# Score matmuls of batches 1 to 3 with a head's q and k on all 128 partitions

## The chip, the cores and the metric

One core of a Trainium2 chip runs one launch. The metric is the device time of the launch in microseconds. Engines are named as the profile names them: PE (matmuls) with PEld (its weight loads), DVE, ACT, POOL, and SP, which only issues DMAs.

## What is computed

Causal attention over 4 batches, 8 heads, 576 tokens, head size 64, all in fp32, with a bias made of running sums, and after it two feed-forward stages over all 2304 tokens:

```python
scores = 0.125 * q @ k.T
cum = np.cumsum(np.maximum(s, 0), axis=-1)
scores = where(causal, -1e9, scores + np.minimum(cum[..., None, :] - cum[..., :, None], 0))
x = softmax(scores) @ v            # heads side by side: 2304 x 512
h = x @ w_in;  x = (h - tanh(h)) @ w_out                 # 512 -> 2048 -> 512
x = ((x @ w1) * (x @ w2)) @ w3 @ w_o2                    # 512 -> 1024 -> 1024 -> 512
```

An fp32 product is made of fp32r matmuls: each operand is cut into a high part (fp32r) and a low part (what is left), and high x high, high x low and low x high are added up in PSUM. In batch 0 the scores are plain fp32 matmuls instead.

## The kernel before

Attention goes by pairs of heads. The two heads of a pair lie on partitions 0 to 63 and 64 to 127, so that one tile `qk` (128 x 2 x 576: q, then k) holds a pair. In batches 1 to 3 each pair of heads is worked off as an early pair (kind A, the first 256 queries, one unit) and a late pair (kind B, the other 320 queries, three units B1, B2, B3); both share one load of q and k. Twelve such couples follow each other. The table `UNITS` (L135) lists what a unit multiplies: A has 128 queries by 128 keys and 128 by 256; B1 and B2 each 96 queries by 512 keys; B3 128 by 384 and 96 by 64.

The order of PE's instructions is written out by hand. `at(step, order, fn)` puts a piece of work into a step, and within a step the pieces come by their order number. A unit's scores have order 4 (L512), its row minimum on DVE order 1 and its exponentials on ACT order 2.5 of the next step; transposes, copies out of PSUM and the products with v follow 7 to 9 steps later. A couple takes 8 steps; its A unit is at step k0, B1 at k0+2, B2 at k0+4, B3 at k0+6. After the attention work of a step come pieces of the first feed-forward stage (`ffn`, its `h` at L452 and `y` at L431), paced so that they fill PE until the next tokens are there. DVE and ACT run in an order that a scheduler chooses, in which `in_turn` keeps some pieces behind others.

For a couple in batches 1 to 3:
- `load` (L170) brings q and k with one DMA of 576 KB on SP's queue, at step k0-6 (L532), held back by `paced` (L148) until the last score matmul before it has ended. It goes into one of five buffers with the tag "raw", taken in turn.
- `cut` (L175) makes the high part on ACT (L178) and the low part on DVE (L179), each with one instruction over 2 x 576 columns, at step k0-3 with order 5.7 (L536). They take two more of the five buffers.
- `scores` (L221) goes for each rectangle of the unit over three passes (high x high, high x low, low x high) and in each over the two heads (L229). Each matmul has 64 rows: head 0 on partitions 0 to 63, head 1 on 64 to 127, into two PSUM banks.

The rings of PSUM banks (`ps_a`, five banks), the biases (`bias`, L192; loaded by `load_cum`, L187, at step k0-5) and everything after the scores stay as they are. Work that the scores share DVE and ACT with: the row minimum (L268), the exponentials (L290), the conversions of weights (`plain`, L84; `park`, L103) and the cutting of the feed-forward input (`cut_x`, L407).

Of the kernel before, what the change touches and what calls it, by code (L numbers as in the profile page):

```python
# [8 lines left out]
F32 = mybir.dt.float32  # L9
F32R = mybir.dt.float32r  # L10
# [5 lines left out]
P = 128  # L16
B, H, S, D = 4, 8, 576, 64
# [7 lines left out]
BLK = 256  # L25
NB = NT // BLK
NSLOT = 16
NP = NH // 2
TAIL = S - BLK

CH0 = [0, 128, 256, 384, 480]
PW = [128, 128, 128, 96, 96]
# [2 lines left out]


@with_exitstack
def tile_kernel(ctx: ExitStack, tc: tile.TileContext, qk, v, s, w_in, w_out, w1, w2, w3t, w_o2, outT):
    nc = tc.nc
    PSUM = bass.MemoryType.PSUM  # L40

# [38 lines left out]
    def in_turn(i, behind):  # L80
        if behind is not None:
            tc.add_manual_dep(i.ins, behind.ins.name, mybir.DependencyInfo(mybir.DependencyClass.NoSync, mybir.DependencyReason.SCHED_ONLY))
# [40 lines left out]
    with ExitStack() as actx:  # L123
        def pool(name, bufs, **kw):
            return actx.enter_context(tc.tile_pool(name=name, bufs=bufs, **kw))

        f2 = pool("f2", 2, reuse_waits="tile")
        a2 = pool("a2", 2, reuse_waits="tile")
# [6 lines left out]
        UNITS = {"A": ((0, 0, P, 0), (1, 0, BLK, P)), "B1": ((3, 0, 512, 0),), "B2": ((4, 0, 512, 0),),  # L135
                 "B3": ((2, 0, 384, 0), (4, 512, S, 384))}
# [8 lines left out]
        latest, least, last_exp, paces = [None], [None], [None], []  # L145
        PACED = 70

        def paced(i):  # L148

            if latest[0] is not None and len(paces) < PACED:  # L150
                paces.append(i)
                tc.add_manual_dep(i.ins, latest[0].ins.name, mybir.DependencyInfo(mybir.DependencyClass.Sync, mybir.DependencyReason.DATA))
            return i

        class Pair:


# [10 lines left out]
                self.nm = self.sums = None  # L168

            def load(self):  # L170
                self.raw = a2.tile([P, 2, S], F32, tag="raw", name=f"qk{self.n}", bufs=5)
                w = BLK if self.first and self.early else S
                return paced(nc.sync.dma_start(self.raw[:, :, :w], qk[self.id, :, :, :w]))

            def cut(self, other):  # L175

                hi, lo = (a2.tile([P, 2, S], F32R, tag="raw", name=f"qk{z}{self.n}", bufs=5) for z in "hl")
                in_turn(nc.scalar.copy(hi, self.raw), last_exp[0])  # L178
                in_turn(nc.vector.tensor_sub(lo, self.raw, hi.bitcast(F32)), least[0])  # L179
                self.hl = other.hl = hi, lo  # L180

            def load_v(self):
                self.vs = a2.tile([P, 2, 5, D], F32, tag="vs", name=f"vs{self.n}", bufs=3)
# [37 lines left out]
        def scores(p, j):  # L221
            ps = [ps_a.tile([P, 512], F32, tag="s", name=f"s{p.n}_{j}_{e}") for e in range(2)]
            p.banks[j] = ps
            for i, k0, k1, o in UNITS[j]:
                passes = ((p.raw, p.raw),) if p.first else ((p.hl[0], p.hl[0]), (p.hl[0], p.hl[1]), (p.hl[1], p.hl[0]))
                for z, (w, x) in enumerate(passes):
                    for e in range(2):
                        r = slice(D * e, D * e + D)
                        latest[0] = nc.tensor.matmul(ps[e][:PW[i], o:o + k1 - k0], w[r, 0, CH0[i]:CH0[i] + PW[i]], x[r, 1, k0:k1],  # L229
                                                     start=z == 0 and (not p.first or (i, k0, k1, o) == UNITS[j][0]),  # L230
                                                     stop=not p.first and z == 2, skip_group_check=True)
            if p.first:


                for e in range(2):
                    g = p.g[e]
                    todo = []
                    for i, k0, k1, o in UNITS[j]:
                        z, r = REL[i]
                        pw, d = PW[i], max(k0, CH0[i])  # L240
                        todo.append((ps[e][:pw, o:o + k1 - k0], pick[:, g:g + 1].broadcast_to([P, pw]), rel2[z][:, r + k0:r + k1]))
                        if d < k1:
                            todo.append((ps[e][:pw, o + d - k0:o + k1 - k0], identb[:, :pw], maskb[:, d - CH0[i]:k1 - CH0[i]]))
                    for z, (o, w, x) in enumerate(todo):
                        nc.tensor.matmul(o, w, x, start=False, stop=z == len(todo) - 1, skip_group_check=True)
# [242 lines left out]
        pairs = [Pair(n, *x) for n, x in enumerate(order)]  # L488
        when = {}

        def at(step, order, fn, *args):
            when.setdefault(step, []).append((order, len(when.get(step, ())), fn, args))
# [8 lines left out]
        start = -2  # L501
        k, avail = 0, []
        for p in pairs:
            n, k0 = p.n, k
            lag = 5 if p.first and p.early else 7
            for m, j in enumerate(p.units):
                k = k0 + 2 * m
                for i in NEED[j]:
                    at(max(k - 2, start), 5, bias, p, i)
                    if not p.first:  # L510
                        at(max(k - 1, start + 1), 0.2, causal, p, i)
                at(k, 4, scores, p, j)  # L512
                at(k + 1, 1, minimum, p, j)
                at(k + 1, 2.5, exps, p, j)
                for e in range(2):
                    at(k + e + lag, 2, transposes, p, j, e)
                    at(k + e + lag + 1, 1.5, evacuate, p, j, e)
                at(k + lag + 2, 8, products, p, j)
            ke = k0 + 2 * len(p.units) - 2
            k = ke + 2  # L520
            at(ke + 2, 5.5, invert, p)
            at(ke + 5, 2.4, turn, p)
            at(ke + 6, 1.2, store, p)
            at(ke + 6, 3.9, spread, p)
            fin = ke + lag + (5 if p.first and p.early else 3)
            at(fin, 2.6, finish, p)
            if p.hp == H // 2 - 1:
                avail.append((S * p.b + (BLK if p.early else S), fin))

            if n > 1 and (p.early or p.first):  # L530
                q = p if p.first else pairs[n + 1]
                at(max(k0 - 6, start + 1), 4.2, load, p, q, "load")  # L532
                at(max(k0 - 2, start + 1), 4.3, load, p, q, "load_v")
                if not p.first:
                    at(k0 - 5, 4.4, load, p, pairs[n + 1], "load_cum")
                    at(k0 - 3, 5.7, p.cut, pairs[n + 1])  # L536


        begin = [next(a for q, a in avail if q >= BLK * (k + 1)) for k in range(NB)]
        step_of, t = [], 0  # L540
        for k in range(NB):
            for i in range(4 * F1):
                t = max(t, begin[k])
# [66 lines left out]
        k = start  # L610
# [227 lines left out]
    for n, f in enumerate(W3ORDER):  # L838
# [3 lines left out]
        ps = ps3.tile([P, 512], F32, tag=f"o{n % 2}", name=f"w3o{f}")  # L842
# [25 lines left out]
    def bank(tag, name, bufs=1):  # L868
        return ps3.tile([P, 512], F32, tag=tag, name=name, bufs=bufs)
# [78 lines left out]
    for u, (sb, f) in enumerate(units):  # L948
# [4 lines left out]
        wu, b = wts.pop(u), bs[sb]  # L953
        nxt = u + 1 < len(units)
        w = bank("W", f"W_{u}", 2)
# [103 lines left out]
```

## Time and profile before

| | |
|---|---|
| time, median of 3 runs | 928.15 us (927.96 to 929.91) |
| the profiled execution | 930.37 us, of which the span of its instructions is 928.6 us |
| PE busy in the span | 913.7 us (98%) |
| PEld, DVE, ACT, POOL | 799.8, 654.3, 447.8, 166.0 us |
| score matmuls of batches 1 to 3 | 87.2 to 334 us of the span |
| granted TensorE clock, mean | 0.998 |

A row of the timeline has the start in us from the start of the span, the time of the group in us, engine, line, operation, tiles, shape and count. The profile draws a matmul from its issue to its modelled end, so that matmuls overlap on PE; what a stream of them takes is read from start to start.

### The profile page before, as it was taken

What the parts mean: (1) busy time and instruction counts of PE and PEld (TensorE: products, weight loads), DVE (VectorE), ACT (ScalarE), POOL (GpSimd) and SP (SyncE); (2) the same over time, 40 slices, a digit from 0 to 9 for tenths busy, and PEclk for the clock granted to TensorE, in tenths of its full rate; (3) what the DMA queues carried; (4) which work ended last, traced back from release to release, by engine and by line L of the source; (5) the groups of instructions that cost most, each with busy time, mean ns of one, the idle gap of its engine ahead of it and who ended that gap; (6) DMA issues with size and microseconds to landing.
All of it is one profiled execution on the core that took longest, in us unless ns stands there. A gap on an engine that the chain in (4) does not pass through costs nothing.

```text
span 928.6 us, 16365 instructions
## 1 busy us (share of the span) xinstructions
PE 913.7 (98%) x6031; PEld 799.8 (86%) x6034; DVE 654.3 (70%) x1445; ACT 447.8 (48%) x1047; POOL 166.0 (18%) x170
## 2 busy tenths in 40 slices
PE   8999999999999999999999999999999999999998
PEld 5567887888888889998888888898999999999998
DVE  8888797877878766867897885767245647564555
ACT  4558888767776743324532342335224333433133
POOL 2015646545344300000000000000011111111100
PEclk9999999999999999999999999999999999999999
DMA  5655365445443523499786635346399777777874
GB/s 162 199 184 167 125 232 189 151 155 163 150 171 126 193 84 100 148 353 378 274 288 228 213 110 164 121 173 223 109 320 316 306 253 284 273 267 257 279 271 151
DMA packets 59936, 192.92 MB, mean 208 GB/s; under 512 B 6640, under 2 KB 21136, under 8 KB 55760
## 3 DMA queue, kind: packets, MB, share of 16 engines
q1 hardware_dynamic: 59856, 191.88, 59.9%
q8 instruction: 47, 0.77, 0.3%
q14 instruction: 33, 0.27, 0.1%
HBM read 148.71 MB, written 43.15 MB: 207 GB/s over the span
## 4 chain that ended last, share of the span: by engine, by line
PE 76%; DMA 4%; DVE 4%; ACT 1%; issue 1%; SPq 0%; DVEq 0%; ACTq 0%
PE W L864 10%; PE y L431 9%; PE h L117 9%; PE yb L117 9%; PE hb L117 8%; PE oW L927 5%; PE Y L864 5%; PE w3o L117 5%; PE oY L927 4%; PE pv L327 3%; PE pt_B L301 2%; PE s_B L229 2%; PE V L864 2%; DMA raw_w<-in_w3t 2%; PE s_A L229 1%
## 5 line engine op out<-in xcount | busy, mean ns | idle before, releaser
L117 PE MATMUL h<-xhl,win 128*128 128x256 f32 x864 | 120.7, 286 | 4.0 <-DVE xhl L65 2.9
L117 PEld LDWEIGHTS h<-xhl,win 128*128 128x128 f32 x864 | 105.9, 188 | 14.5 <-DVE xhl L65 3.6
L117 PE MATMUL hb<-x,win 128*128 128x512 f32 (+1 forms) x480 | 104.6, 367 | 0.0
L117 PEld LDWEIGHTS hb<-x,win 128*128 128x128 f32 x480 | 83.9, 188 | 14.9
L117 PE MATMUL yb<-ghb,wout 128*128 128x512 f32 (+1 forms) x320 | 96.1, 368 | 0.7 <-ACT ghb L64 0.5
L997 POOL TENSOR_TENSOR xy<-c,c 128x384 f32<-128x384 f32 x12 | 15.4, 1279 | 445.1 <-DVE c L986 445.1
L206 POOL TENSOR_SCALAR pr<-cb,cq 128x384 f32<-128x384 f32 (+1 forms) x48 | 91.2, 1912 | 13.4 <-PE s_B L229 7.6
L431 PE MATMUL y<-gh,wout 128*128 128x256 f32 x576 | 86.1, 290 | 0.4 <-DVE gh L64 0.4
L290 ACT ACTIVATE pr<-pr,nm 128x128 f32<-128x128 f32 (+2 forms) x120 | 71.4, 597 | 20.8 <-DVE nm L268 20.7
L431 PEld LDWEIGHTS y<-gh,wout 128*128 128x128 f32 x576 | 73.3, 191 | 3.6 <-issue 2.0
L117 PEld LDWEIGHTS yb<-ghb,wout 128*128 128x128 f32 x320 | 58.2, 188 | 11.2 <-ACT ghb L64 1.3
L117 PE MATMUL yb<-glb,wout 128*128 128x512 f32 (+1 forms) x160 | 58.6, 368 | 0.2 <-DVE glb L65 0.2
L301 PE MATMUL pt_B<-ident,pr 96*128 96x96 f32 (+1 forms) x384 | 51.6, 257 | 0.1
L268 DVE CUSTOM_DVE_ANT_0 pr<-s_B,pr 96x512 f32<-96x512 f32 (+1 forms) x72 | 44.4, 637 | 9.3 <-PE s_B L229 8.3
L218 POOL TENSOR_SCALAR_AFFINE_SELECT pr<-pr 128x256 f32<-128x256 f32 (+2 forms) x60 | 30.0, 520 | 98.3 <-issue 97.8
L64 ACT CAST ghb<-thb 128x512 fp32r<-128x512 f32 (+1 forms) x40 | 23.1, 579 | 50.3 <-DVE thb L726 50.3
L310 ACT COPY pf_B<-pt_B 128x512 f32<-128x512 f32 (+2 forms) x72 | 35.8, 499 | 20.9 <-PE pt_B L301 20.6
L460 ACT ACTIVATE th<-h 128x256 f32<-128x256 f32 x72 | 26.9, 374 | 38.7 <-PE h L117 37.6
L431 PE MATMUL y<-gl,wout 128*128 128x256 f32 x288 | 45.2, 280 | 0.0
L301 PEld LDWEIGHTS pt_B<-ident,pr 96*128 96x128 f32 (+1 forms) x384 | 41.1, 142 | 4.4 <-issue 3.0
L875 ACT COPY s<-Y 128x384 f32<-128x384 f32 x24 | 11.6, 482 | 63.6 <-PE Y L864 61.1
L463 DVE TENSOR_TENSOR th<-h,th 128x256 f32<-128x256 f32 x72 | 30.0, 416 | 15.0 <-ACT th L460 14.3
(217 smaller groups left out, 2045.1 us busy)
## 6 DMA issues: line engine op xcount, KB each, us to landing
S<-wg_d SPq DMA_DIRECT2D x24, 1024.0 KB
wo<-wo_d SPq DMA_DIRECT2D x42, 512.0 KB
A<-wg_d SPq DMA_DIRECT2D x24, 768.0 KB
qk<-in_qk SPq DMA_DIRECT2D x16, 576.0 KB
raw_win<-in_w_in SPq DMA_DIRECT2D x16, 512.0 KB
raw_wout<-in_w_out SPq DMA_DIRECT2D x16, 512.0 KB
raw_w<-in_w SPq DMA_DIRECT2D x16, 512.0 KB
wg_d<-pks SPq DMA_DIRECT2D x8, 1024.0 KB
```

The costliest lines, as they stand in the source:

```text
L117: i = nc.tensor.matmul(ps, a, b, start=first and n == 0, stop=last and n == 2, skip_group_check=skip)
L206: nc.gpsimd.tensor_scalar(out=t[:pw, e, :w], in0=p.cb[:pw, e, :w], scalar1=c, scalar2=0.0, op0=ALU.add, op1=ALU.min)
L218: nc.gpsimd.affine_select(out=dg, in_=dg, pattern=[[0, 2], [-1, w - c]], compare_op=ALU.is_ge, fill=-8e9, base=0, channel_multiplier=1)
L268: least[0] = nc.vector.tensor_tensor_reduce(out=t[:pw, k0:k1], in0=ps[:pw, o:o + k1 - k0], in1=t[:pw, k0:k1], scale=-0.125, scalar=nm[:pw, ...
L290: last_exp[0] = nc.scalar.activation(t[:pw, :], t[:pw, :], AF.Exp, bias=m, scale=-1.0, accum_out=p.sums[:pw, e, c:c + 1])
L301: nc.tensor.transpose(pt[:, at:at + pw], p.pr[i][:pw, e, KC0[kj]:KC0[kj] + P], ident[:pw, :pw])
L310: (nc.vector.tensor_copy if j == "B2" and not p.first else nc.scalar.copy)(pf[:, :at], pt[:, :at])
L327: nc.tensor.matmul(p.pv[D * e:D * e + D, c:p.nq], p.vs[:, e, kj], pf[:, beg:end], start=z == 0, stop=z == len(todo) - 1, skip_group_check= ...
L431: nc.tensor.matmul(o, wout[f][:, z, P * c:P * c + P], x, start=f == 0 and n == 0 and c % 2 == 0, stop=f == F1 - 1 and n == 2, skip_group_c ...
L463: nc.vector.tensor_sub(t, hh, t)
L864: i = nc.tensor.matmul(ps[:, :T], w[:, x, P * j:P * j + P], b[:, y, j], start=first and j == n == 0, stop=stop and j == 1 and n == 2, skip ...
L927: nc.tensor.matmul(ps[:, :T], w[:, a, q % 2, P * j:P * j + P], x[:, b, q], start=o in ("B11", "B21", "T1") and q == z == 0, stop=o in ("T4 ...
```

## The change

The host lays out a second input `qd` for batches 1 to 3: for each pair of heads and for q and k one array of 128 x 2 x 576, in which head e stands in [:, e, :], its 64 rows twice, on partitions 0 to 63 and again on 64 to 127. `load` brings q and k in two DMAs of 576 KB into the tiles `qr` and `kr`. `cut` makes three tiles: `qh` (high part of q, on both halves), `ql` (low part of q, on both halves) and `ks` (high part of k on partitions 0 to 63, low part on 64 to 127; ACT writes the high part on all partitions, then DVE puts the low part over the upper half). A matmul of all 128 rows of `qh` with `ks` gives high x high plus high x low; one of `ql` with `ks` gives low x high plus low x low. Each head and rectangle has these two matmuls. The five tiles have one buffer each. The cut goes in two parts: columns 0 to 255 at step k0-2, and columns 256 to 575 at step k0, both with order 5.7.

```diff
-                self.raw = a2.tile([P, 2, S], F32, tag="raw", name=f"qk{self.n}", bufs=5)
-                w = BLK if self.first and self.early else S
+                if not self.first:
+                    self.raw = [place(t, f"{t}{self.n}") for t in ("qr", "kr")]
+                    for z, t in enumerate(self.raw):
+                        i = paced(nc.sync.dma_start(t, qd[self.id - H // 2, z]))
+                    return i
+                self.raw = place(("qr", "kr", "qh", "ks", "ql")[self.n % 5], f"qk{self.n}")
+                w = BLK if self.early else S
...
-            def cut(self, other):
-                hi, lo = (a2.tile([P, 2, S], F32R, tag="raw", name=f"qk{z}{self.n}", bufs=5) for z in "hl")
-                in_turn(nc.scalar.copy(hi, self.raw), last_exp[0])
-                in_turn(nc.vector.tensor_sub(lo, self.raw, hi.bitcast(F32)), least[0])
-                self.hl = other.hl = hi, lo
+            def cut(self, other, a, b):
+                (qr, kr), c = self.raw, slice(a, b)
+                if not a:
+                    self.hl = other.hl = [place(t, f"{t}{self.n}", F32R) for t in ("qh", "ks", "ql")]
+                qh, ks, ql = self.hl
+                in_turn(nc.scalar.copy(qh[:, :, c], qr[:, :, c]), last_exp[0])
+                in_turn(nc.vector.tensor_sub(ql[:, :, c], qr[:, :, c], qh[:, :, c].bitcast(F32)), least[0])
+                in_turn(nc.scalar.copy(ks[:, :, c], kr[:, :, c]), last_exp[0])
+                in_turn(nc.vector.tensor_sub(ks[D:, :, c], kr[D:, :, c], ks[D:, :, c].bitcast(F32)), least[0])
...
+                    for z in (0, 2):
+                        latest[0] = nc.tensor.matmul(ps[e][:PW[i], o:o + k1 - k0], p.hl[z][:, e, CH0[i]:CH0[i] + PW[i]], p.hl[1][:, e, k0:k1],
+                                                     start=z == 0, stop=z == 2, skip_group_check=True)
...
-                    at(k0 - 3, 5.7, p.cut, pairs[n + 1])
+                    at(k0 - 2, 5.7, p.cut, pairs[n + 1], 0, BLK)
+                    at(k0, 5.7, p.cut, pairs[n + 1], BLK, S)
```

`place` takes a tile of 128 x 2 x 576 with one buffer under the given tag. Batch 0 keeps its scores; its pairs take the same five places in turn.

## Rows read from the trace of the kernel before

**Rows 1.** Page, part 1: busy time, share of the span, instructions.
```profile
PE 913.7 (98%) x6031; PEld 799.8 (86%) x6034; DVE 654.3 (70%) x1445; ACT 447.8 (48%) x1047; POOL 166.0 (18%) x170
```
**Rows 2.** Windows of one couple: length, busy PE PEld DVE ACT POOL, clock, DMA; sum.
```profile
162.40:186.40 24.00, 22.54 (x182) 19.03 (x180) 20.08 (x60) 17.72 (x49) 12.73 (x12) 0.93 0.44 146
...
sum 252.80, PE 249.71 PEld 209.46 DVE 200.47 ACT 188.81 POOL 120.03; mean PE 20.81 PEld 17.45 DVE 16.71 ACT 15.73 POOL 10.00
```
**Rows 3.** Waits of PE, 20 to 345 us: total us, times, longest.
```profile
PE h L117 <- DVE xhl L65: 2.9, 2, 1.5
```
**Rows 4.** Timeline of PE around a unit B2 and a unit B3.
```profile
97.44 0.52 PE L301 MATMUL pt_B<-ident,pr 128*128 128x128 f32 x4
97.90 0.48 PE L229 MATMUL s_B<-qkh 64*96 64x512 f32 x2
98.21 0.40 PE L229 MATMUL s_B<-qkl,qkh 64*96 64x512 f32 x2
98.45 0.40 PE L229 MATMUL s_B<-qkh,qkl 64*96 64x512 f32 x2
98.78 0.97 PE L431 MATMUL y<-gh,wout 128*128 128x256 f32 x6
...
101.05 0.44 PE L229 MATMUL s_B<-qkh 64*128 64x384 f32 x2
...
101.70 0.25 PE L229 MATMUL s_B<-qkl,qkh 64*96 64x64 f32 x2
101.78 0.25 PE L229 MATMUL s_B<-qkh,qkl 64*96 64x64 f32 x2
101.97 1.69 PE L117 MATMUL h<-xhl,win 128*128 128x256 f32 x12
```
**Rows 5.** Timeline of PE around a unit A, in two windows.
```profile
208.25 0.33 PE L229 MATMUL s_A<-qkh 64*128 64x128 f32 x2
...
208.53 0.27 PE L229 MATMUL s_A<-qkh,qkl 64*128 64x128 f32 x2
...
209.13 0.38 PE L117 MATMUL h<-xhl,win 128*128 128x256 f32 x1
...
209.35 1.46 PE L117 MATMUL h<-xhl,win 128*128 128x256 f32 x11
210.65 0.60 PE L301 MATMUL pt_B<-ident,pr 128*128 128x128 f32 x5
211.04 1.17 PE L431 MATMUL y<-gh,wout 128*128 128x256 f32 x8
```
**Rows 6.** Timeline of PE: streams of 128-row matmuls in later stages.
```profile
449.98 2.88 PE L117 MATMUL hb<-x,win 128*128 128x512 f32 x12
452.70 0.39 PE L117 MATMUL yb<-ghb,wout 128*128 128x512 f32 x1
...
700.43 1.20 PE L864 MATMUL Y<-B22hl,S 128*128 128x384 f32 x6
701.47 0.85 PE L864 MATMUL W<-T3hl,S 128*128 128x384 f32 x4
```
**Rows 7.** Groups: busy us, mean ns of one, idle before, its releaser.
```profile
L178 ACT CAST qkh<-qk 128x1152 fp32r<-128x1152 f32 x12 | 13.8, 1154 | 7.6 <-DMA qk<-in_qk 7.6
L179 DVE TENSOR_TENSOR qkl<-qk,qkh 128x1152 fp32r<-128x1152 f32 x12 | 16.2, 1350 | 0.0
...
L64 ACT CAST ghb<-thb 128x512 fp32r<-128x512 f32 x32 | 19.9, 622 | 45.0 <-DVE thb L726 45.0
...
L65 DVE TENSOR_TENSOR glb<-thb,ghb 128x512 fp32r<-128x512 f32 x32 | 22.0, 688 | 6.5 <-ACT ghb L64 6.2
```
**Rows 8.** Windows between units: A to B1 (first, last), B3 to A (middle).
```profile
163.30:166.80 3.50, 3.50 (x34) 2.92 (x32) 3.43 (x16) 1.93 (x8) 2.66 (x5) 1.00 0.02 5
290.35:296.37 6.02, 6.02 (x53) 4.70 (x51) 4.43 (x16) 4.43 (x12) 6.02 (x4) 1.00 0.68 235
297.25:302.10 4.85, 4.85 (x44) 4.29 (x42) 4.62 (x19) 3.74 (x13) 1.15 (x5) 1.00 0.01 3
```

More of the change, by code (lines that the diff above doesn't have):

```diff
@@ L37, in tile_kernel @@
 @with_exitstack
-def tile_kernel(ctx: ExitStack, tc: tile.TileContext, qk, v, s, w_in, w_out, w1, w2, w3t, w_o2, outT):
+def tile_kernel(ctx: ExitStack, tc: tile.TileContext, qk, qd, v, s, w_in, w_out, w1, w2, w3t, w_o2, outT):
     nc = tc.nc
@@ L153, in paced, with place @@
             return i
+        def place(tag, name, dt=F32):
+            return a2.tile([P, 2, S], dt, tag=tag, name=name, bufs=1)
         class Pair:
@@ L224, in scores @@
             for i, k0, k1, o in UNITS[j]:
-                passes = ((p.raw, p.raw),) if p.first else ((p.hl[0], p.hl[0]), (p.hl[0], p.hl[1]), (p.hl[1], p.hl[0]))
-                for z, (w, x) in enumerate(passes):
-                    for e in range(2):
+                for e in range(2):
+                    if p.first:
                         r = slice(D * e, D * e + D)
-                        latest[0] = nc.tensor.matmul(ps[e][:PW[i], o:o + k1 - k0], w[r, 0, CH0[i]:CH0[i] + PW[i]], x[r, 1, k0:k1],
-                                                     start=z == 0 and (not p.first or (i, k0, k1, o) == UNITS[j][0]),
-                                                     stop=not p.first and z == 2, skip_group_check=True)
+                        latest[0] = nc.tensor.matmul(ps[e][:PW[i], o:o + k1 - k0], p.raw[r, 0, CH0[i]:CH0[i] + PW[i]], p.raw[r, 1, k0:k1],
+                                                     start=(i, k0, k1, o) == UNITS[j][0], stop=False, skip_group_check=True)
+                        continue
+                    for z in (0, 2):
+                        latest[0] = nc.tensor.matmul(ps[e][:PW[i], o:o + k1 - k0], p.hl[z][:, e, CH0[i]:CH0[i] + PW[i]], p.hl[1][:, e, k0:k1],
+                                                     start=z == 0, stop=z == 2, skip_group_check=True)
             if p.first:
@@ L1039 @@
     qk = np.stack([q, k], axis=2).reshape(NP, 2, 2, S, D).transpose(0, 1, 4, 2, 3)
+    qd = np.stack([q, k], axis=1).reshape(B, 2, H // 2, 2, S, D)[1:].transpose(0, 2, 1, 5, 3, 4).reshape(NP - H // 2, 2, D, 2, S)
     arrays = {
         "qk": np.ascontiguousarray(qk).reshape(NP, P, 2, S),
+        "qd": np.ascontiguousarray(np.stack([qd, qd], axis=2)).reshape(NP - H // 2, 2, P, 2, S),
         "v": vp,
```

## Prediction

> **What bounds the kernel now.** I read the page first: PE is busy 913.7 of 928.6 us, no other engine above 71% beside its own weight loads [rows 1]. Then the windows by couple, over the stretch that the change touches: in 252.8 us PE is busy 249.7, DVE 200.5, ACT 188.8 [rows 2]. PE is the bound here, its order is written by hand, and a microsecond of PE time saved is a microsecond of the span so long as the others keep up. DVE keeps 52 us free there, ACT 64. PE's few waits show what happens where they don't: the longest (1.5 us, for DVE's cut of the feed-forward input) [rows 3] lies in the couple in which PE is busy 22.54 of 24.00 us and the mean granted clock is 0.93 [rows 2]. A stretch there ran at the lower level, 1.2 instead of 2.4 GHz, after PE had stood idle. Seven per cent of 24 us is 1.7 us lost beside the wait. Last the timeline of PE: what a unit's scores really take.
>
> **How the scores run now.** In B2 the three passes start at 97.90, 98.21 and 98.45 us, two matmuls in each [rows 4]. So a pass of both heads takes 0.24 us, and one matmul of 512 columns over all 128 rows takes 2.72/12 = 0.227 us [rows 6]. The two heads, on different halves of the array, run side by side: a pass of two costs what one full matmul costs.
>
> The Trainium skill, TensorEngine Tiling (Array Packing), section Performance Considerations, advises just this for a contraction of 64 rows or less: tile the rows, two matmuls at once. The trace agrees inside the unit. By that rule alone the change is a loss: four matmuls one after the other where there were three passes. Its time is worked out as a rival below.
>
> But the halves have an edge. Four transposes ahead of B2 take 97.44 to 97.90, 0.46 us [rows 4]; five ahead of full matmuls take 210.65 to 211.04, 0.39 [rows 5]. One transpose is some 0.08 (0.39/5), so going to half-array matmuls costs 0.46 - 4 x 0.08 - the same 0.03 or so, thus **0.15 us**, taken low 0.12. At the other end the last pass of B2 takes 98.45 to 98.78, 0.33 instead of 0.24 (in the block below), and the first full matmul after a unit 209.13 to 209.35, 0.22, where the next eleven take 1.30/11 = 0.118 [rows 5]: **0.10 us** more. The same page (section Key Properties) says that a change of tiling mode drains the engine. These rows fit that, though they show the time and not its cause.
>
> **PE, step by step.** Before, a unit costs 0.15 (entry) + its block from its first score to the next work + 0.10 (exit). Blocks: B1 and B2 0.88, B3 0.92 (101.05 to 101.97) [rows 4], A 0.88 (208.25 to 209.13) [rows 5]. That makes 1.13, 1.13, 1.17 and 1.13 us.
> After, all matmuls around are full ones and entry and exit fall away. What stays is the longer first interval after transposes, 0.07 (0.31 against 0.24 in B2 [rows 4]). Prices from start to start: 512 columns 0.227, 384 columns 1.04/6 = 0.173 [rows 6], 256 columns 0.118 [rows 5]. Two operations have no full-array row. For 128 columns the three passes of A go from 208.25 to 208.53, 0.28; less 0.07, that is 0.105 each [rows 5]. For 64 columns the pass from 101.70 to 101.78 gives 0.08 [rows 4]. I take both; they could be as low as 0.06 and 0.04 if the columns alone counted (by the 0.118 of 256), and as high as 0.118 each.
> - B1, B2: 4 x 0.227 + 0.07 = 0.98, saves 0.15 each.
> - B3: 4 x 0.173 + 4 x 0.08 + 0.07 = 1.08, saves 0.09.
> - A: 4 x 0.118 + 4 x 0.105 + 0.07 = 0.96, saves 0.17.
>
> Together 0.56 a couple, twelve couples: **-6.7 us**. Rounding of starts to 0.01 us, and the low entry of 0.12, put it between -5.3 and -7; with the first interval's 0.07 gone too (48 x 0.07 = 3.4) and the small matmuls at their lowest (12 x 4 x 0.085 = 4.1) the far end is -14, with them at their highest (12 x 4 x 0.05 = 2.4) the near end is -2.9. I take -6.5.
>
> **ACT and DVE.** The cut now goes over q and k twice. ACT: 512 columns 0.622 us, 1152 columns 1.154 [rows 7], so 0.83 ns a column and 0.73 us for 640. Two of each are 2.70 instead of 1.15: +1.55 x 12 = **+18.6 us on ACT**. DVE: 0.688 and 1.350 [rows 7], 0.82 for 640, 3.02 instead of 1.35: **+20 us on DVE** (half of its instructions go over 64 partitions, which I count as no cheaper). Both fit into the 64 and 52 us that are free, so the sum puts them at nothing; the cover is that slack, and in places it is thin.
>
> **Waits that the change adds.** With one buffer, part 1 of the cut (256 columns of each head) cannot start before B3 of the couple before has left the three tiles, and A waits for it. The chain is ACT 0.62, ACT 0.62, DVE 0.69 = 1.93 us, in a stretch of 6.02 in which ACT and DVE each have 1.59 free [rows 8]: the added 1.24 and 1.38 fit. Part 2 (320 columns) comes after A and B1 waits for it: 0.73 + 0.73 + 0.82 = 2.28 us, in 4.85 with DVE 4.62 busy, and at the tightest 3.50 with DVE 3.43 [rows 8]. Here 1.64 us of DVE work finds 0.23 or 0.07 free. Behind the waiting instructions on DVE stand A's row minimum, which frees PSUM banks, and the conversions, which can wait. Since the cut is issued ahead of the conversions of its step, I expect it to push those back and PE to be held seldom. If nothing gave way, B1 would be late by 1.64 - 0.23 = 1.4 us, twelve times: 17 us. If everything did, nothing. I take **+2 us**, near the lower end since the chain of 2.28 fits twice into 4.85; that is one late B1 in nine, or one of 1.5 us with the clock's 1.7 on top.
>
> **DMA and SP.** Twelve more DMAs of 576 KB: at 146 GB/s for a share of 0.44 [rows 2] the full rate is some 330 GB/s, so 1.7 us each. The load still goes at k0-6, the first part needs it at k0-2 instead of k0-3; a step is about 2.6 us (252.8/96 [rows 2]), so the later step pays for it. ACT waited 7.6 us in all for these loads [rows 7], and that wait goes. Late next is the bias of the couple, queued behind: 1.7 us later, ACT waits there. Counted at nothing on PE for the same slack, at most part of the 17 us above.
>
> **Sum.** -6.5 + 2 = -4.5 us. The profiled execution took 930.37 us, 0.24% over the median of 928.15; the saving carries over, so about 925.9 there and **923.7 us** as the median.
>
> **Rivals.**
> 1. *The cut becomes the wait* (slower). Place: B1, behind part 2 of the cut on DVE, in the stretch from A. For it: DVE is 95% busy there [rows 8]. Against: conversions can be pushed back, and DVE is only 79% busy over all. Price: up to 17 us, so 928.15 - 6.5 + 17 = 939. It decides from 6.5/12 = 0.54 us a couple on. Chance 0.14.
> 2. *Side by side is worth more than the edges cost* (slower). If what entry and exit cost belongs to the scores and not to the halves, 0.25 stays in each unit, and a fourth matmul comes on top: B1, B2 +0.23 each, B3 +0.25, A +0.22, together 0.93 x 12 = 11 us: 939. This is what the skill's advice gives. Against: the exit of full matmuls to full matmuls costs nothing extra in the streams [rows 6]. Chance 0.05.
> 3. *The gain is taken back* by small waits of PE on DVE, ACT or PSUM banks: 6.5 us lost over 24 parts of a cut, 0.27 each: 926.3 to 930, no change. Chance 0.19.
> 4. *It doesn't do what it says* (the cut parts queue so that both A and B1 see the old rhythm, PE idles at unchanged step times): the same time as 3, counted there.
>
> **Numbers.** My forecast, faster by over 0.2% (1.9 us, about what a measurement of this kernel can tell from no change), has 0.62, from 918 to 926 by itself. No change 0.19, slower 0.19 (rivals 1 and 2). To leave out no more than 2 in 10, the range goes from 919 to 932: below lie the lowest prices of the small matmuls, above the harder half of rivals 1 and 2.
>
> **What the profile would show.** Right: score matmuls 128 rows high, starting one by one; B1's block near 0.98 us; the first matmul after a unit as quick as the second; PE's windows over the twelve couples shorter by 5 to 7 us; DVE busy near 220 us there, ACT near 207. Wrong: PE waiting at s_B or s_A for DVE's `ks` or `ql`, at transposes for a copy that ACT made late, a second stretch at the lower clock, or full-array scores that keep an entry of 0.15 us.

## The result, and the profile after

The changed kernel takes **938.84 us** (median of 6 runs, 934.76 to 942.48); the kernel before took 927.54 beside it (6 runs, 925.57 to 929.91). The ratio is 1.0115, 95% interval 1.0096 to 1.0133: **slower by 10.7 us**, where 4.5 us faster was forecast. The profiled execution has a span of 937.9 us against 928.6.

The page's first part, of the changed kernel: PE is busy as long as before [rows 1], DVE 20 us and ACT 15 us longer.

```profile
PE 913.0 (97%) x5890; PEld 810.8 (86%) x5890; DVE 674.0 (72%) x1481; ACT 463.1 (49%) x1083; POOL 172.1 (18%) x170
```

The stretch from the first to the last score matmul of batches 1 to 3, as windows (length, busy PE PEld DVE ACT POOL, granted clock, DMA share, GB/s). First the kernel before:

```profile
87.20:333.90 246.70, 243.60 (x2115) 204.63 (x2116) 198.72 (x604) 185.72 (x510) 120.03 (x120) 0.99 0.47 159
```

And the changed kernel; the last two are two short windows in its third couple:

```profile
86.50:344.20 257.70, 244.63 (x1971) 215.39 (x1971) 218.87 (x639) 200.19 (x545) 127.65 (x121) 0.98 0.52 177
129.00:132.00 3.00, 0.06 (x1) 0.09 (x2) 1.43 (x4) 3.00 (x9) 3.00 (x2) 0.94 0.51 135
131.60:135.10 3.50, 3.16 (x16) 3.19 (x17) 3.37 (x8) 2.13 (x6) 3.50 (x3) 0.51 0.44 157
```

The stretch is 11.0 us longer, more than the whole loss of the profiled execution. PE stands idle 13.1 us in it (257.70 - 244.63) instead of 3.1. And the clock costs more: after the idle of 3 us at 129 the next 3.5 us ran at 0.51, the level of 1.2 GHz. Two more stretches of the changed kernel ran at that level, each after PE had stood idle in places; the kernel before had one. First the one of before, then the two:

```profile
171.00:174.40 3.40, 3.40 (x19) 3.40 (x18) 1.64 (x4) 1.89 (x6) 0.00 (x0) 0.50 0.94 330
```
```profile
179.40:182.80 3.40, 3.40 (x20) 3.40 (x19) 1.74 (x5) 1.76 (x5) 0.00 (x0) 0.51 1.03 411
...
261.40:264.80 3.40, 3.23 (x15) 3.24 (x16) 3.30 (x6) 2.67 (x7) 3.40 (x6) 0.50 0.54 161
```

At half the full clock, 3.4 us cost 1.7 us of work: 1.7 us lost before, 5.1 after.

Now the score matmuls themselves, in the timeline of PE (two windows of the changed kernel), to be held against [rows 4] and [rows 5]:

```profile
96.54 0.53 PE L315 MATMUL pt_B<-ident,pr 128*128 128x128 f32 x4
96.85 0.45 PE L244 MATMUL s_B<-ks,qh 128*96 128x512 f32 x1
97.14 0.39 PE L244 MATMUL s_B<-ks,ql 128*96 128x512 f32 x1
97.36 0.39 PE L244 MATMUL s_B<-ks,qh 128*96 128x512 f32 x1
97.59 0.40 PE L244 MATMUL s_B<-ks,ql 128*96 128x512 f32 x1
97.82 0.85 PE L445 MATMUL y<-gh,wout 128*128 128x256 f32 x6
...
99.83 0.42 PE L244 MATMUL s_B<-ks,qh 128*128 128x384 f32 x1
...
100.90 1.66 PE L117 MATMUL h<-xhl,win 128*128 128x256 f32 x12
102.40 0.49 PE L315 MATMUL pt_A<-ident,pr 128*128 128x128 f32 x3
...
107.24 0.33 PE L244 MATMUL s_A<-ks,qh 128*128 128x128 f32 x1 [0.92 <-DVE ks L192]
107.40 0.28 PE L244 MATMUL s_A<-ks,ql 128*128 128x128 f32 x1
107.52 0.28 PE L244 MATMUL s_A<-ks,qh 128*128 128x128 f32 x1
...
108.27 0.39 PE L445 MATMUL y<-gh,wout 128*128 128x256 f32 x2
```

The entry is gone: four transposes ahead of B2 take 0.31 us (96.54 to 96.85) instead of 0.46. B2's block is 0.97 (0.98 forecast), B3's 1.07 (1.08), A's 1.03 (0.96). Only after B3 a little of the exit stays: twelve `h` take 1.50 us from 100.90 to 102.40, 0.08 more than twelve at 0.118. So a couple saves 0.16 in B1 and in B2, 0.02 in B3 and 0.10 in A, some **5 us** for twelve. PE got what it was to get. The waits and the clock took it, and twice as much again.

What PE waited for, from the first score to the last (total us, times, longest):

```profile
PE pt_B L315 <- DVE xy L378: 3.0, 1, 3.0
PE h L117 <- DVE xhl L65: 2.8, 3, 1.1
PE s_A L244 <- DVE ks L192: 2.7, 3, 0.9
PE h L117 <- DVE th L477: 2.0, 3, 0.9
```

One wait of 3.0 us, the others at most 1.1, and only 2.7 us of them for the cut itself. The wait of 0.92 us at 107.24 (second couple) comes behind a slow instruction on DVE, whose `ql` of 512 columns took 1.25 us there and 0.68 to 0.69 elsewhere at its fastest:

```profile
105.22 1.25 DVE L190 TENSOR_TENSOR ql<-qr,qh 128x512 fp32r<-128x512 f32 x1
106.50 0.69 DVE L192 TENSOR_TENSOR ks<-kr,ks 64x512 fp32r<-64x512 f32 x1
```

What the others waited for, in the same stretch:

```profile
POOL pr L218 <- DMA cb<-cum_d: 49.0, 5, 14.6
...
ACT pr L220 <- DMA cb<-cum_d: 11.0, 8, 3.3
...
SPq L177 <- PE s_B L244: 35.0, 10, 4.8
SPq L177 <- DVE ql L190: 30.6, 7, 6.1
```

Before, ACT waited 3.0 us for the couple's bias `cb`, and POOL did not wait for it. The 49 us are not new idle time, though: all of POOL's waits together are 119.5 us now and 112.8 before, then put down to other releasers. The same holds for SP's queue, which stands at the load of q and k (L177) for 65.6 us, 30.6 of them put down to DVE's reading of the old tiles. Before, it stood at that load nearly as long, for PE alone:

```profile
SPq L173 <- PE s_B L229: 59.6, 10, 9.6
```

`paced` holds the load until the last score matmul of B1 anyway, and DVE had read the old tiles by then. One couple, from that matmul to the first reading of the bias, before and after:

```profile
131.08 0.40 PE L229 MATMUL s_B<-qkh,qkl 64*96 64x512 f32 x2
131.55 0.33 SPq L173 DMA_DIRECT2D qk<-in_qk  x1
131.97 0.38 SPq L190 DMA_DIRECT2D cb<-cum_d  x1
136.73 1.50 ACT L208 ACTIVATE pr<-cb,cq 128x256 f32<-128x256 f32 x4 [0.25 <-DMA cb<-cum_d]
```
```profile
137.84 0.39 PE L244 MATMUL s_B<-ks,ql 128*96 128x512 f32 x1
138.25 0.33 SPq L177 DMA_DIRECT2D qr<-in_qd  x1
138.63 0.42 SPq L177 DMA_DIRECT2D kr<-in_qd  x1
139.16 0.38 SPq L202 DMA_DIRECT2D cb<-cum_d  x1
144.89 1.50 ACT L220 ACTIVATE pr<-cb,cq 128x256 f32<-128x256 f32 x4 [1.19 <-DMA cb<-cum_d]
```

The load goes out within 0.1 us of the matmul's end in all of eleven couples before and in ten of eleven after; in the eleventh it is 1.45 us late, and the queue had stood at a store of converted weights (L106) just ahead of it. So the single buffers hold the queue in none. The bias lands late all the same, since one more load is issued and moved ahead of it: 8.4 us after that matmul instead of 6.6, as means over the eleven couples.

DVE's and ACT's cut, by shape (line, operation, count, busy, mean ns, idle before), against [rows 7]:

```profile
L190 DVE TENSOR_TENSOR ql<-qr,qh 128x640 fp32r<-128x640 f32 x12 | 11.6, 966 | 0.1
L192 DVE TENSOR_TENSOR ks<-kr,ks 64x512 fp32r<-64x512 f32 x12 | 10.8, 902 | 0.4
L192 DVE TENSOR_TENSOR ks<-kr,ks 64x640 fp32r<-64x640 f32 x12 | 10.8, 897 | 0.4
L190 DVE TENSOR_TENSOR ql<-qr,qh 128x512 fp32r<-128x512 f32 x12 | 10.1, 844 | 4.7 <-ACT qh L189 4.7
```

DVE spends 43.3 us on it instead of 16.2: +27, where +20 was reckoned. ACT spends 32.0 us on its 48 instructions instead of 13.8: +18.2, where +18.6 was reckoned.

### The profile page after: what moved, and what is told of

It reads as the page before. It is cut to its first block, busy times and chain, and to the rows that moved or that the text cites. A ratio compares the mean times of both kernels' runs of the same rounds, so it can differ in the third digit from the quotient of the medians.

```text
span 937.9 us, 16234 instructions
## 1 busy us (share of the span) xinstructions
PE 913.0 (97%) x5890; PEld 810.8 (86%) x5890; DVE 674.0 (72%) x1481; ACT 463.1 (49%) x1083; POOL 172.1 (18%) x170
## 4 chain that ended last, share of the span: by engine, by line
PE 76%; DVE 8%; DMA 7%; ACT 5%; issue 3%; POOL 1%; SPq 1%; ACTq 0%; DVEq 0%; POOLq 0%
PE hb L117 10%; PE yb L117 10%; PE W L879 10%; PE y L445 8%; PE h L117 7%; PE oW L942 5%; PE Y L879 5%; PE w3o L117 5%; PE oY L942 4%; DMA cb<-cum_d 3%; PE pv L341 3%; PE V L879 2%; PE pt_B L315 2%; PE s_B L244 2%; DMA rd<-rt 1%
## 5 line engine op out<-in xcount | busy, mean ns | idle before, releaser
L117 PEld LDWEIGHTS h<-xhl,win 128*128 128x128 f32 x864 | 108.6, 190 | 11.6 <-DVE xhl L65 4.8
L218 POOL TENSOR_SCALAR pr<-cb,cq 96x512 f32<-96x512 f32 (+1 forms) x48 | 92.3, 1937 | 61.7 <-DMA cb<-cum_d 49.0
L230 POOL TENSOR_SCALAR_AFFINE_SELECT pr<-pr 128x256 f32<-128x256 f32 (+2 forms) x60 | 33.8, 591 | 59.9 <-issue 35.9
L220 ACT ACTIVATE pr<-cb,cq 128x256 f32<-128x256 f32 (+2 forms) x72 | 34.9, 553 | 11.0 <-DMA cb<-cum_d 11.0
```

The lines of the kernel that those rows point to most:

```text
L117: i = nc.tensor.matmul(ps, a, b, start=first and n == 0, stop=last and n == 2, skip_group_check=skip)
L218: nc.gpsimd.tensor_scalar(out=t[:pw, e, :w], in0=p.cb[:pw, e, :w], scalar1=c, scalar2=0.0, op0=ALU.add, op1=ALU.min)
L220: nc.scalar.activation(t[:pw, e, :w], p.cb[:pw, e, :w], AF.Identity, bias=c)
L230: nc.gpsimd.affine_select(out=dg, in_=dg, pattern=[[0, 2], [-1, w - c]], compare_op=ALU.is_ge, fill=-8e9, base=0, channel_multiplier=1)
```

## The experiments

Five candidates: the price of full matmuls, the added **work** on ACT and DVE, the **wait of A** for the first part of the cut, the **loads**, behind which the bias comes late, and whether a saving on PE reaches the end at all. All ratios are to the kernel before, run on the same chip, with the 95% interval.

**Full rows, old loads and cut.** Edit to the kernel before:

```diff
+                    for z in (0, 1):
+                        latest[0] = nc.tensor.matmul(ps[e][:PW[i], o:o + k1 - k0], p.hl[z][:, 0, CH0[i]:CH0[i] + PW[i]], p.hl[1 - z][:, 1, k0:k1],
+                                                     start=z == 0, stop=z == 1, skip_group_check=True)
```

> The kernel before with its loads and its cut, but scores by four matmuls of 128 rows a rectangle (they add up both heads, so the scores are other numbers). All theories agree on the PE side alone: no entry and exit of half-array matmuls, 5 to 7 us less, 920.5 to 922.5 us. If the price of full-array matmuls were what made the change slow, it would stay at 927.5 or above.

Measured: 928.99 us, 0.9993 (0.9968 to 1.0017). No gain, and no loss: the 5 to 7 us forecast here did not come. So full matmuls don't make the change slow, yet their saving hardly arrives even without the new cut. In its profile PE's busy time over the scores' stretch is 239.2 us (before: 243.6), but PE waits:

```profile
PE h L117 <- DVE th L465: 2.0, 2, 1.3
PE y L433 <- POOL gl L65: 1.9, 1, 1.9
```

The first feed-forward stage fills PE between the scores, and its operands come from ACT, DVE and POOL. When PE is quicker, it stands before them.

**Old matmuls, new loads and cut.**

```diff
+                passes = ((p.raw, p.raw),) if p.first else ((p.hl[0], p.hl[1]), (p.hl[0], p.hl[1]), (p.hl[2], p.hl[1]))
+                for z, (w, x) in enumerate(passes):
+                    for e in range(2):
+                        r = slice(D * e, D * e + D)
+                        c, d = (0, 1) if p.first else (e, e)
+                        latest[0] = nc.tensor.matmul(ps[e][:PW[i], o:o + k1 - k0], w[r, c, CH0[i]:CH0[i] + PW[i]], x[r, d, k0:k1],
```

> The changed kernel with its loads and cut, but scores by three passes of 64 rows over the two heads side by side, as before (one pass takes the wrong part of k, so the scores are other numbers). If the new loads and cut are what cost, PE's saving is missing and their cost stays: 942 to 946 us. If the longer PE time of full matmuls were the cost, 928.

Measured: 947.76 us, 1.0203 (1.0165 to 1.0241), a little above the range given. The loads and the cut cost some 19 us; the full rows give back 8 of them (1.0203 to 1.0115), part of it clock (means of 0.987 to 0.994 here, 0.992 to 0.998 in the changed kernel). All the loss is theirs.

**Cut in place, no score waits for it.**

```diff
+                if self.n == 8 and not a:
+                    cuts.append([place(t, f"{t}{self.n}", F32R) for t in ("qh", "ks", "ql")])
+                self.hl = other.hl = cuts[0]
+                qh, ks, ql = cuts[0] if self.n == 8 else (qr, kr, qr)
```

> The changed kernel, but from the second couple on ACT and DVE do their four instructions of a part in place on the loaded tiles, and the scores read the first couple's cut (other numbers). ACT and DVE do as much, the loads wait as long, but no score waits for a cut. Theory 'A waits for the first part' (single buffers, cut only after B3): 922 to 927 us. Theory 'the load waits for the second part and holds the bias behind it': still 933 to 938. Theory 'DVE and ACT have too much to do': still 933 to 938.

Measured: 937.31 us, 1.0090 (1.0053 to 1.0126). Taking away the wait of A alone changes nothing that the intervals can tell. The theory that it is the main cause falls.

**One load.**

```diff
+                    if raws:
+                        self.raw = raws[0]
+                        return
```

> The changed kernel, but only the first couple's q and k are loaded, and every couple cuts these (other numbers); the cut's work and the wait of A for it stay. Theory 'the load waits for the second part and holds the bias behind it on SP': most of the loss gone, 923 to 929 us, and POOL's wait for the bias (49 us in all) under 10. Theory 'A waits for the first part': still 933 to 938.

Measured: 933.01 us, 1.0052 (1.0027 to 1.0077): more than half of the loss is gone, with all of the cut's work and A's wait still there. POOL no longer waits for the bias; PE still does for `ks`, 1.2 us. The time is above the 929 given as the upper end, so the loads are not all.

**Half the cut.** `ks` is not made, and the scores take `qh` as moving.

```diff
-                in_turn(nc.scalar.copy(ks[:, :, c], kr[:, :, c]), last_exp[0])
-                in_turn(nc.vector.tensor_sub(ks[D:, :, c], kr[D:, :, c], ks[D:, :, c].bitcast(F32)), least[0])
```

> The changed kernel without ks: ACT and DVE cut q alone (two instructions each a part less: as much work as before the change), and the scores take qh as the moving operand (other numbers); loads, single buffers and the two steps stay. Theory 'DVE and ACT have too much to do': ratio to before 0.997 to 1.001, near that of full rows with the old cut (0.999). Theory 'the loads hold SP's queue': half of the loss stays, 1.004 to 1.008, since the loads still wait for the second part.

Measured: 930.93 us, 1.0007 (0.9988 to 1.0026). With ACT and DVE doing about as much as before, the loss is gone, though loads, single buffers and steps are the new ones. And the bias is as late as in the changed kernel (8.2 us after B1's last score matmul on average, against 8.4), with POOL waiting for it as long:

```profile
POOL pr L216 <- DMA cb<-cum_d: 51.8, 5, 12.8
```

So late loads and a late bias by themselves cost nothing that can be told (1.0007 against 0.9993 for full rows with the old loads and cut). The run also makes the chain in front of A shorter, but taking A's wait away alone left 1.0090. What is left for the loss is the added work: without it there is none.

**Work alone**: both waits taken away by the two edits above, one load and the cut in place.

> The changed kernel with both waits taken away: q and k loaded once, and from the second couple on ACT and DVE do their four instructions of a part in place, and no score waits for them (other numbers). Only the added work on ACT and DVE is left. Theory 'too much work': 1.004 to 1.008, no better than one load with the wait of A kept (1.0052). Theory 'the loads, and the rest is A's wait': 0.997 to 1.001.

Measured: 932.76 us, 1.0023 (1.0004 to 1.0042), below what "too much work" gave and above what "the loads" gave. Against full rows with the old cut (0.9993) that is 2.8 us for the added work without a late bias and without A's wait, at the edge of what the intervals tell apart. From here to one load (A's wait comes back) it is 2.7 us, to the cut in place (the loads come back) 6.2. So on top of the added work the loads do cost.

**Bias first.** The same computation as the changed kernel.

```diff
-                    at(k0 - 5, 4.4, load, p, pairs[n + 1], "load_cum")
+                    at(k0 - 6, 4.1, load, p, pairs[n + 1], "load_cum")
```

> The changed kernel with the couple's bias loaded one step earlier, ahead of q and k in SP's queue; the same computation. Theory 'the late loads hold the bias, and the late bias holds POOL and ACT': 1.003 to 1.007 instead of 1.0115, POOL waiting for the bias under 10 us instead of 49. Theory 'too much work on ACT and DVE': no change, 1.009 to 1.013.

Measured: 934.66 us, 1.0061 (1.0032 to 1.0090). POOL's waits in its profile, from the first score to the last:

```profile
POOL pr L230 <- issue: 82.0, 9, 11.8
POOL pr L218 <- PE pt_B L315: 18.5, 9, 4.0
```

The wait for the bias is not among them (ACT still waits 17.4 us for it). The bias lands 5.0 us after B1's last score matmul, 3.4 earlier than in the changed kernel. Some 5 us come back by moving one DMA ahead of two others, about as many as by having no loads at all. How much of the 3.4 us is the bytes ahead of it, and how much the place in the queue, these runs don't part.

One rival stays open for this run, one load and work alone: each edit lets the scheduler order DVE and ACT anew. Of the changed kernel's order of ACT's other instructions between the scores, half the cut keeps 92% and the cut in place 93%, but bias first 66%, one load 64% and work alone 47% (by the matching stretches of the two sequences). What the new order itself gives or takes was not measured.

**Bias first, part of the cut on POOL.**

```diff
-                in_turn(nc.vector.tensor_sub(ks[D:, :, c], kr[D:, :, c], ks[D:, :, c].bitcast(F32)), least[0])
+                in_turn((nc.gpsimd if a else nc.vector).tensor_sub(ks[D:, :, c], kr[D:, :, c], ks[D:, :, c].bitcast(F32)), least[0])
```

> As the run before, and the low part of k in the second part of the cut made on POOL instead of DVE (12 instructions of 640 columns); the same computation. Theory 'too much work on DVE': better by 3 to 5 us than with the bias first alone, if POOL, which is 43% busy there, gets to them in time. Theory 'loads': the same as with the bias first.

Measured: 935.75 us, 1.0064 (1.0038 to 1.0090). No better. But POOL did not get to them in time, so the run says little about DVE's work:

```profile
PE s_B L244 <- POOL ks L192: 4.5, 2, 3.1
```

**Full rows, nothing cut**, from the second couple on, and its **control** with the old matmuls.

```diff
+                if cuts:
+                    self.hl = other.hl = cuts[0]
+                    return
```

> Full rows with the old loads, and the cut made for the first couple only (eleven cuts of 1.15 us on ACT and 1.35 us on DVE left out, other numbers; three buffers for the loads). Theory 'the saving of PE is lost because ACT and DVE lag': with less on them it arrives, 0.992 to 0.996. Theory 'full rows save nothing on PE': 0.998 to 1.001 again.

> The control: the kernel before with the cut made for the first couple only, and the same three buffers. Theory 'PE alone bounds the kernel before': 0.998 to 1.001, and the run above 5 us under this one. Theory 'ACT and DVE are as near the bound as PE': 0.994 to 0.997 here already.

Measured: 923.77 us, **0.9943** (0.9925 to 0.9962) with full rows, and 927.73 us, **0.9990** (0.9971 to 1.0009) with the old ones. The control says that taking 25 us of work off ACT and DVE does nothing for the old kernel: PE bounds it. Beside it, full rows give 4 us, most of the 5 that the timeline showed. The windows from the first to the last score, full rows first, then the control:

```profile
87.30:327.60 240.30, 236.98 (x1974) 210.46 (x1972) 184.79 (x593) 174.49 (x499) 113.94 (x120) 1.00 0.50 163
```
```profile
88.80:334.60 245.80, 242.18 (x2115) 203.04 (x2115) 184.44 (x593) 173.91 (x499) 112.84 (x120) 1.00 0.49 160
```

PE busy is 5.2 us less, and the stretch 5.5 us shorter: here a microsecond of PE is a microsecond of the span.

**One wait for POOL moved to DVE**, with the old cut, and with the bias first.

```diff
-                            split(gh, gl, t)
+                            split(gh, gl, t, lo=nc.vector.tensor_sub)
```

> Full rows with the old loads and cut (other numbers), and for the first 256 tokens the low part of the feed-forward's operand on DVE instead of POOL, where it stood behind biases and held PE for 1.9 us. If single waits like this one eat the saving, 0.996 to 0.998; if the lag only moves to DVE, 0.999 to 1.001.

> The changed kernel with the bias first and the same move from POOL to DVE; the same computation. With the bias first alone it was 1.006. If the one wait of 3.1 us and the clock's drop after it go, 1.001 to 1.004; if the lag only moves, 1.005 to 1.008.

Measured: 927.54 us, 0.9983 (0.9965 to 1.0002), and 934.50 us, 1.0065 (1.0041 to 1.0089). The wait of `y` for POOL is gone from both profiles; the second has a wait of 2.3 us for DVE's `xhl` instead. The first result lies between its two forecasts, the second is what was forecast for a lag that moves. No version that computes the reference beat the kernel before, and the most that full rows won in any run is the 4 us above.

## Why the prediction was wrong

- **PE, step by step: right**, a third too large. -6.7 was reckoned (-6.5 taken); the timeline after gives about -5, and the pair with nothing cut -4 in time. The term for B2 holds to 0.01 us; A's eight matmuls took 0.07 longer than reckoned, and B3 kept 0.08 of its exit. The entry was right by luck: 0.46 - 4 x 0.08 - 0.03 is 0.11 and not 0.15, but 0.15 is what the timeline after shows (0.46 - 0.31). Rival 2, that side by side is worth more than its edges, fell: the entry vanished with the half-array matmuls. That agrees with the Trainium skill, TensorEngine Tiling (Array Packing), section Key Properties, by which changing the mode drains the engine; 0.15 us in and 0.10 out is what it cost here. The advice of the Trainium skill on the same page, section Performance Considerations, to tile the rows for short contractions did not decide here.
- **"Both fit into the 64 and 52 us that are free, so the sum puts them at nothing"** is the step that failed. With half the cut left out, so that ACT and DVE had about as much to do as before, the loss was gone (1.0007 instead of 1.0115), with the loads, the single buffers and the late bias all kept. By itself, without late bias and without A's wait, the work cost some 3 us; together with them the loss is the whole 10.7. The size of the work was short too (DVE +27 instead of +20).
- **"A microsecond of PE time saved is a microsecond of the span so long as the others keep up"**: true with the cut left out (0.9943 against 0.9990), nearly void with the old cut in place (0.9993). The condition was the point. DVE's 52 us free over the stretch said nothing of the moments in which PE stands before `h` and `y`.
- **"Late next is the bias of the couple ... Counted at nothing on PE for the same slack"**: the delay was right, the price leaned on the slack that failed. 1.7 us later was reckoned, 1.8 measured. ACT's wait for it went from 3.0 to 11.0 us. Without the added work the late bias cost nothing that can be told (1.0007); with it, having the bias early gave back some 5 us (1.0115 to 1.0061), though that run also changed the order on ACT and DVE.
- **"Waits that the change adds: +2 us"**: the chain was worked out, yet put at B1. PE waited for `ks` at A (2.7 us in the profile), and never at B1 for the cut. Its cost in time is some 2.7 us (1.0023 to 1.0052), at the edge of the intervals. That the first part fits into 1.59 us of free time took DVE's prices for granted: in the second couple `ql` took 1.25 us instead of 0.69, and A waited 0.92.
- **The clock** was priced for one more idle stretch and not summed up. In the profiled executions it cost 5.1 us over the scores instead of 1.7. A second stretch at the lower clock was among the prediction's own signs of being wrong. Whether full rows by themselves make the clock fall more often is not shown: the mean granted clock was 0.998 or more in 12 of 12 runs of each kernel without the cut and in 4 of 10 with full rows and the old cut, against 40 of 54 runs of the kernel before beside them and 8 of 12 with one wait moved; and in the profiled execution with full rows and the old cut the stretches at the lower level lay outside the scores (at 36 and 589 us).
- **Rival 1** had the right sign and, by chance, the right time (939). It is the nearest of the rivals, since DVE has too little time there, but its mechanism, B1 waiting behind the second part, was not what happened.

The parts can be added up along one path: with full rows and the old cut -0.6 us, +2.8 for the work, +2.7 for A's wait and +6.2 for the loads give 11.1; measured are 10.7. But the first three are no larger than their uncertainty, and they are not prices that hold by themselves: the same loads with half the cut stand at 1.0007. Not settled is how the loss divides between ACT and DVE, and how much of it goes by way of the late bias.

## What to carry over

Where one engine is 98% busy and the order is fixed, check first that a saving on it reaches the end: leave out the work of its suppliers, with and without the change, and compare the pair. Slack summed over a long stretch hides nothing if the work falls due at certain moments, and two things that are each covered by the same slack can cost together what neither costs alone. A wait that the profile puts down to a new releaser need not be new: look at what the instruction waited for before, and when it went out.

## What was not expected of the hardware

An instruction over 64 partitions costs DVE as much as one over 128: 897 ns on average for 640 columns, 966 for the full height (above). And the same 640 columns took 0.82 us in one place and 1.01 in another. In the timeline of DVE (changed kernel), and of POOL beside it:

```profile
89.85 0.82 DVE L190 TENSOR_TENSOR ql<-qr,qh 128x640 fp32r<-128x640 f32 x1
...
128.70 1.01 DVE L190 TENSOR_TENSOR ql<-qr,qh 128x640 fp32r<-128x640 f32 x1
```
```profile
88.84 6.22 POOL L218 TENSOR_SCALAR pr<-cb,cq 96x512 f32<-96x512 f32 x3
...
127.96 4.35 POOL L218 TENSOR_SCALAR pr<-cb,cq 96x512 f32<-96x512 f32 x2 [14.58 <-DMA cb<-cum_d]
```

POOL was at the biases in both cases, so that alone doesn't tell them apart. Over all 48 instructions of DVE's cut the trace says a little more. The five that ran with POOL idle, or all but idle, took 0.68 to 0.69 us for 512 columns and 0.82 for 640. The 32 that took longer (0.83 to 1.33 us, and 0.86 to 1.14) all ran beside POOL for a third of their time or more, but 11 others beside POOL were as short. The twelve cuts of the kernel before took 1.34 to 1.36 us whether POOL ran or not. So what lengthens DVE's instructions here stays open; the 7 us by which DVE's cut was undersized come from it.
